# A fourth block product of an MLP layer split into seven smaller ones, on one core of a Trainium2 chip

## Chip, cores and metric

The kernel runs on one core of a Trainium2 chip. The metric is the time of one execution on the device in microseconds (us). Before the change three runs gave 829.02, 829.6 and 1758.81 us; the median is 829.6. The profile comes from a further execution of 829.24 us, with a span of 827.5 us from the first to the last instruction and a mean granted TensorE clock of 0.999.

## What is computed

An attention whose mask comes from a clustering (a query sees the keys of its own cluster), over 4 batches, 8 heads, 768 tokens and a head width of 64. Its output, 768 x 512 per batch, goes through an MLP mixer:

```python
def _moe_ref(x, w_tok1, w_tok2, w_ch1, w_ch2) -> np.ndarray:
    xt = x.transpose(0, 2, 1)
    h = np.maximum(xt @ w_tok1, 0.0) @ w_tok2      # tokens: 768 -> 256 -> 768
    u = x + h.transpose(0, 2, 1)
    h2 = np.maximum(u @ w_ch1, 0.0) @ w_ch2        # channels: 512 -> 1536 -> 512
    return (u + h2).astype(np.float32)
```

All of it is float32. The change concerns `u @ w_ch1`, the first channel product, in which 512 channels become 1536.

## The kernel before

The large products are made by Winograd's form of Strassen's scheme: both matrices are cut into 2 x 2 blocks, and seven block products stand in for eight. Sums of blocks (S1 to S4 of the left matrix, T1 to T4 of the right one) go in, and partial sums of the seven products come out. In the table, a product has the PSUM bank that it is summed up in, its two factors, and the output block that takes the bank's contents once the product is in:

```python
SEVEN = {
    "p1": ("X", "A11", "B11", "c11"),
    "p5": ("Z", "S1", "T1", "c22"),
    "c11": ("Y", "A12", "B21", "c11"),
    "u2": ("X", "S2", "T2", "c12"),
    "c12": ("Z", "S4", "B22", "c12"),
    "c22": ("X", "S3", "T3", "c22"),
    "c21": ("X", "A22", "T4", "c21"),
}
# ...
def winograd_right(b):
    yield lambda: sub(b["T1"], b["B12"], b["B11"])
    yield lambda: sub(b["T2"], b["B22"], b["T1"])
    yield lambda: sub(b["T3"], b["B22"], b["B12"])
    yield lambda: sub(b["T4"], b["B21"], b["T2"])
```

In the first channel product the left matrix is the weight, the right one is `u`, turned, so a block product is 256 channels deep and 384 tokens wide. The work is done in twelve *pairs* (four batches, three parts): a pair makes 128 rows of the upper and 128 rows of the lower half of each block (`i` is 0 or 1) by `ch1_pair`, and then the second channel product takes them in (`ch2_chunks`: 21 chunks of two matmuls of 256 columns). A whole ("big") block product of a pair is two rows x two halves of the depth, four matmuls of 384 columns. In all pairs but the first, three of the seven block products (Y = A12 B21, Z = S4 B22, X = A22 T4) are *set* products: each is cut once more, by the same table, into seven matmuls of 192 columns whose outputs are put together in SBUF.

A big product works in a bank; a chain such as Y's p1, u2, c22, c21 adds one small product after another into the same bank, and after each of them VectorE adds the bank to an output in SBUF before the next may be added to the bank.

```python
def big(psum, a, r, i, start):
    product(psum, a, r, i, start)                  # two matmuls of 384 columns
    between()                                      # hands out work that waits: sums, late chains
    if a != "A11" and beside:
        beside.pop(0)()                            # turning of the next batch's u
def set_(psum, which, name, start):                # one matmul of 192 columns
    # ...
def set_x(which, tag, name, x):
    if tag:
        chains[which] = ptile(tag, HS // 2)
    bank = chains[which]
    set_(bank, which, name, name == "p1")
    add(x, both(bank) if len(x.shape) == 3 else bank, x)
# ...
for i in range(2):
    X[i] = ptile("X", HS)
    big(X[i], "A11", "B11", i, True)
    nc.scalar.copy(out=a11[:, i], in_=X[i])
# ... (Z[0] = S1 T1, copied to p5 by ScalarE; Y's direct products c11 and c12; Y's p1)
Z[1] = ptile("Z", HS)
big(Z[1], "S1", "T1", 1, True)
nc.scalar.copy(out=p5[:, 1], in_=Z[1])
# ... (Y's u2 and p5; X[0] += S2 T2, copied to u2; Y's c22; Z's c11, c12 into Z[0])
big(X[1], "S2", "T2", 1, False)
nc.scalar.copy(out=u2[:, 1], in_=X[1])
set_x("Y", None, "c21", a11[:, 1, n0])
relu(a11)                                          # ScalarE, 768 wide
set_(Z[1][:, n0], "Z", "c21", False)
add(c12[:, 0], Z[0], u2[:, 0])
set_x("Z", "Z", "p1", c12[:, 0, n0])
add(c12[:, 1], Z[1], u2[:, 1])
big(X[0], "S3", "T3", 0, False)
add(a22[:, 0], X[0], p5[:, 0])
set_x("Z", None, "u2", c12[:, 0, n1])
set_z("Z", ptile("Y", HS // 2), c12)               # Z's p5
big(X[1], "S3", "T3", 1, False)
add(a22[:, 1], X[1], p5[:, 1])
relu(a22)
set_x("Z", None, "c22", c12[:, 1].rearrange("p (k t) -> p k t", k=2))
# ... (X's products c11, c12, c21 into X[0] and X[1], copied to a12; X's p1)
sum_1()                                            # then the second product begins;
late.extend([late_1, late_2])                      # X's u2, p5 and c22 run between its chunks
```

[...]three with the tag X, three with Z, two with Y. The kernel sets the order of the instructions on each engine itself: they stand as they are written.

Of the kernel before, what the change touches and what calls it, by code (L numbers as in the profile page):

```python
# [19 lines left out]
P = 128  # L20
# [8 lines left out]
HS = HJ * P  # L29
# [21 lines left out]
def kernel(  # L51
# [497 lines left out]

    SEVEN = {  # L550
# [16 lines left out]
    def left_weights():  # L567

        w = W["ch1"]
        half = DCH // 2  # L570
        A = pools["A"] = {
            f"A{i + 1}{j + 1}": w[:, 2 * j : 2 * j + 2, half * i : half * i + half]
            for i in range(2)
            for j in range(2)
        }
        extra = pools["wsums"].tile([P, 3, 2, half], F32, name="w1s")
        A["S1"], A["S2"], A["S4"] = (extra[:, i] for i in range(3))
        A["S3"] = A["A21"]
# [22 lines left out]
    def set_lefts():  # L601
        if "l2" not in pools:
            pools["l2"] = pools["w2sums"].tile([P, 3, 3, HS], F32, name="w1ss")
        A, l2 = pools["A"], pools["l2"]
        both = W["ch1"].rearrange("p f (i r c) -> p f i r c", i=2, r=2)[:, 2:4]
        single = A["S4"].rearrange("p f (r c) -> p f r c", r=2)
        for blocks, sums_ in (
            ([both[:, f, :, r] for r in range(2) for f in range(2)], [l2[:, 0:2, m] for m in range(3)]),
            ([single[:, f, r] for r in range(2) for f in range(2)], [l2[:, 2, m] for m in range(3)]),
        ):  # L610
            yield dict(
                zip(("A11", "A12", "A21", "A22", "S1", "S2", "S4", "S3"), blocks + sums_ + blocks[2:3])
            )
# [6 lines left out]
    def set_rights():  # L620
        uT, t4, r2 = pools["uT"], pools["R"]["T4"], pools["r2"]
        both = uT[:, :, 2:4].rearrange("p n f (k t) -> p n f k t", k=2)
        single = t4.rearrange("p f (k t) -> p f k t", k=2)
        for blocks, sums_ in (
            ([both[:, :, f, k] for f in range(2) for k in range(2)], [r2[:, 0:2, m] for m in range(3)]),
            ([single[:, f, k] for f in range(2) for k in range(2)], [r2[:, 2, m] for m in range(3)]),
        ):
            yield dict(
                zip(("B11", "B12", "B21", "B22", "T1", "T2", "T4", "T3"), blocks + sums_ + blocks[1:2])
            )  # L630

    def set_right_sums():
        pools["r2"] = pools["w2sums"].tile([P, 3, 3, HS // 2], F32, name="uTss")
        for blocks in set_rights():
            yield from winograd_right(blocks)

    def set_blocks():

        (yx, z), (yz, x) = (list(y) for y in (set_lefts(), set_rights()))
        left = {"Y": {k: a[:, 0] for k, a in yx.items()}, "X": {k: a[:, 1] for k, a in yx.items()}, "Z": z}  # L640
        right = {"Y": {k: b[:, 0] for k, b in yz.items()}, "Z": {k: b[:, 1] for k, b in yz.items()}, "X": x}
# [141 lines left out]
    def ch1_pair(part, sets, beside):  # L783
# [6 lines left out]
        p5, u2, c12 = (pools["mlp"].tile([P, 2, HS], F32, name=k) for k in ("p5", "u2", "c12"))  # L790
        A, R = pools["A"], pools["R"]
        left, right = set_blocks() if sets else (None, None)
        n0, n1 = slice(0, HS // 2), slice(HS // 2, HS)
        X, Y, Z, chains = {}, {}, {}, {}
# [15 lines left out]
        def set_(psum, which, name, start):  # L810
# [6 lines left out]
        def both(psum):  # L817
            return psum.unsqueeze(1).to_broadcast([P, 2, HS // 2])

        def relu(x):  # L820
            nc.scalar.activation(out=x, in_=x, func=ACT.Relu)  # L821


        def set_x(which, tag, name, x):
            if tag:
                chains[which] = ptile(tag, HS // 2)
            bank = chains[which]
            set_(bank, which, name, name == "p1")
            add(x, both(bank) if len(x.shape) == 3 else bank, x)

        def set_z(which, bank, x):
            set_(bank, which, "p5", True)
            add(x[:, :, n1], both(bank), x[:, :, n1])

        a11, a12, a22 = h2["A11"], h2["A12"], h2["A22"]
        for i in range(2):
            X[i] = ptile("X", HS)
            big(X[i], "A11", "B11", i, True)
            nc.scalar.copy(out=a11[:, i], in_=X[i])  # L839
        Z[0] = ptile("Z", HS)  # L840
        big(Z[0], "S1", "T1", 0, True)
        nc.scalar.copy(out=p5[:, 0], in_=Z[0])
        if sets:
            yc = ptile("X", HS)
            set_(yc[:, n0], "Y", "c11", True)
            set_(yc[:, n1], "Y", "c12", True)
            add(a11[:, 0], yc, a11[:, 0])
            set_x("Y", "Y", "p1", a11[:, 0, n0])
        Z[1] = ptile("Z", HS)
        big(Z[1], "S1", "T1", 1, True)  # L850
        nc.scalar.copy(out=p5[:, 1], in_=Z[1])
        if sets:
            set_x("Y", None, "u2", a11[:, 0, n1])
            set_z("Y", ptile("Y", HS // 2), a11)
        else:
            Y[0] = ptile("Y", HS)
            big(Y[0], "A12", "B21", 0, True)
            add(a11[:, 0], Y[0], a11[:, 0])
        big(X[0], "S2", "T2", 0, False)
        nc.scalar.copy(out=u2[:, 0], in_=X[0])  # L860
        if sets:
            set_x("Y", None, "c22", a11[:, 1, n1])
            set_(Z[0][:, n0], "Z", "c11", False)
            set_(Z[0][:, n1], "Z", "c12", False)
        else:
            Y[1] = ptile("Y", HS)
            big(Y[1], "A12", "B21", 1, True)
            add(a11[:, 1], Y[1], a11[:, 1])
        big(X[1], "S2", "T2", 1, False)
        nc.scalar.copy(out=u2[:, 1], in_=X[1])  # L870
        if sets:
            set_x("Y", None, "c21", a11[:, 1, n0])
            relu(a11)
            set_(Z[1][:, n0], "Z", "c21", False)
            add(c12[:, 0], Z[0], u2[:, 0])
            set_x("Z", "Z", "p1", c12[:, 0, n0])
            add(c12[:, 1], Z[1], u2[:, 1])
        else:
            relu(a11)
            big(Z[0], "S4", "B22", 0, False)  # L880
            add(c12[:, 0], Z[0], u2[:, 0])
        big(X[0], "S3", "T3", 0, False)
        add(a22[:, 0], X[0], p5[:, 0])
        if sets:
            set_x("Z", None, "u2", c12[:, 0, n1])
            set_z("Z", ptile("Y", HS // 2), c12)
        else:
            big(Z[1], "S4", "B22", 1, False)
            add(c12[:, 1], Z[1], u2[:, 1])
# [3 lines left out]
        if sets:  # L893
            set_x("Z", None, "c22", c12[:, 1].rearrange("p (k t) -> p k t", k=2))
            set_(X[0][:, n0], "X", "c11", False)
            set_(X[0][:, n1], "X", "c12", False)
            nc.scalar.copy(out=a12[:, 0], in_=X[0])  # L897
            set_(X[1][:, n0], "X", "c21", False)
            nc.scalar.copy(out=a12[:, 1], in_=X[1])


        def sum_3():
            nc.vector.scalar_tensor_tensor(
                out=h2["S3"], in0=c12, scalar=0.0, in1=a11, op0=ALU.max, op1=ALU.subtract
            )

        def sum_1():
            nc.vector.scalar_tensor_tensor(
                out=h2["S1"], in0=c12, scalar=0.0, in1=a22, op0=ALU.max, op1=ALU.add
            )  # L910

        def sum_4():
            sub(h2["S4"], a12, h2["S2"])

        if sets:
            set_x("X", "Y", "p1", a12[:, 0, n0])
            sum_1()

            def late_1():
                set_x("X", None, "u2", a12[:, 0, n1])  # L920
                set_z("X", ptile("Z", HS // 2), a12)
                sub(h2["S2"], h2["S1"], a11)

            def late_2():
                set_x("X", None, "c22", a12[:, 1].rearrange("p (k t) -> p k t", k=2))
                relu(a12)
                sum_3()
                sum_4()

            late.extend([late_1, late_2])  # L930
        else:
            sum_1()

            def late_(i):
                product(X[i], "A22", "T4", i, False)
                nc.scalar.activation(out=a12[:, i], in_=X[i], func=ACT.Relu)
                if i == 0:
                    sub(h2["S2"], h2["S1"], a11)
                else:
                    sum_3()  # L940
                    sum_4()

            late_(0)
            late.append(lambda: late_(1))
# [214 lines left out]
    for n, b in enumerate(batches):  # L1159
        turning = []  # L1160
        for part in range(3):
# [9 lines left out]
            if first:  # L1171
                others += list(set_right_sums()) + list(right_weights(1))
# [8 lines left out]
            if part == 2 and not last:  # L1181
                after[3] = lambda: take(turning, len(turning))
                after[15] = lambda: next(usums)
                usums = u_sums()
            ch2_chunks(b, part, last, after)
# [3 lines left out]
            if part == 2 and not last:  # L1189

                steps = list(set_right_sums())
                for m in range(2):
                    steps[m]()
                next(usums)
# [217 lines left out]
```

## Time and profile before

| what | value |
|---|---|
| time, median | 829.6 us |
| span of the profile | 827.5 us |
| TensorE busy | 818.1 us, 99% |
| VectorE busy | 605.3 us, 73% |
| ScalarE busy | 381.6 us, 46% |
| the line of the big first-channel products, L799, pX from uT | 192 records, 487 ns each |
| ReLU of the hidden blocks, L821, 768 wide | 35, 843 ns each |
| copy of a bank of 384 to SBUF, L839 | 24, 479 ns each |
| one pair with its second product, in the middle of the second batch | 35.34 us (536.86 to 572.20) |

The attention takes the first part of the span, the two channel products some 430 us at its end. In the profile, PE is TensorE, DVE VectorE, ACT ScalarE. A line number is that of the kernel before; L799 is a big product, L812 a small one, L952 the second channel product, L565 VectorE's adds, L562 its subtractions. A float32 matmul stands in the trace as two records. Matmuls are pipelined, so the length of one record is longer than the distance to the next; distances between starts tell what one costs.

### The profile page before, as it was taken

The numbers are of one execution on the slowest core, as the hardware profiler recorded it, in microseconds if no ns is written. First come the engines' busy times: TensorE is split into PE (matmuls) and PEld (weight loads), VectorE is DVE, ScalarE is ACT, GpSimd is POOL, SyncE is SP. The second block draws the span as 40 slices with busy tenths as digits, with TensorE's granted clock in tenths as the row PEclk, the third lists the DMA queues.
The fourth block names the chain that finished last, engine by engine and source line by source line (L and its number), as shares of the span: only waits on it lengthen the run. The fifth ranks groups of instructions, "written<-read, shape, count | busy, mean of one in ns | idle before, by whom it ended". The sixth has DMA issues, their size and how long they took to land.

```text
span 827.5 us, 11453 instructions
## 1 busy us (share of the span) xinstructions
PE 818.1 (99%) x4282; PEld 526.0 (64%) x4282; DVE 605.3 (73%) x1124; ACT 381.6 (46%) x562; POOL 30.6 (4%) x28
## 2 busy tenths in 40 slices
PE   8999999999999999999999999999999999999996
PEld 4444444444444444444688787878878788787875
DVE  6879898989898968859777687654677456674654
ACT  5588777787878775136202253121541214512020
POOL 1001010111101000000000000000000000000000
PEclk9999999999999999999999999999999999999999
DMA  8787676777776434143000114000130001400002
GB/s 155 141 165 145 124 141 121 160 138 154 140 155 140 84 96 121 51 156 48 0 1 1 29 34 168 1 0 15 35 105 1 1 1 30 123 1 0 1 2 80
DMA packets 184256, 63.39 MB, mean 77 GB/s; under 512 B 172800, under 2 KB 176896, under 8 KB 183936
## 3 DMA queue, kind: packets, MB, share of 16 engines
q1 hardware_dynamic: 182592, 62.18, 34.4%
q8 instruction: 35, 0.57, 0.3%
q10 hardware_dynamic: 1600, 0.39, 0.2%
q14 instruction: 29, 0.24, 0.1%
HBM read 36.21 MB, written 7.86 MB: 53 GB/s over the span
## 4 chain that ended last, share of the span: by engine, by line
PE 95%; DVE 4%; ACT 0%; issue 0%; ACTq 0%; DVEq 0%
PE sc L413 19%; PE av L455 15%; PE pX L952 14%; PE pX L799 11%; PE pZ L952 7%; PE ph L534 5%; PE pY L812 4%; PE pY L952 4%; PE pZ L799 3%; PE pZ L812 3%; PE pX L773 2%; PE pX L812 2%; PE small L491 2%; PE pZ L773 1%; PE small L304 1%; DVE hA L565 1%
## 5 line engine op out<-in xcount | busy, mean ns | idle before, releaser
L437 ACT ACTIVATE ex<-sc 128x768 f32<-128x768 f32 x192 | 151.0, 812 | 27.2 <-PE sc L413 15.5
L413 PE MATMUL sc<-qkT 64*128 64x384 f32 x768 | 155.3, 483 | 0.0
L445 DVE TENSOR_TENSOR sum<-sum,ex 128x768 f32<-128x768 f32 x128 | 127.8, 999 | 27.3 <-ACT ex L437 15.2
L455 PE MATMUL av<-ex,va 128*64 128x384 f32 x768 | 127.4, 488 | 0.0
L565 DVE TENSOR_TENSOR x<-pX,x 128x256 f32<-128x256 f32 (+1 forms) x168 | 76.2, 461 | 40.9 <-PE pX L952 40.4
L455 PEld LDWEIGHTS av<-ex,va 128*64 128x64 f32 x768 | 53.7, 137 | 71.7 <-issue 67.8
L413 PEld LDWEIGHTS sc<-qkT 64*128 64x128 f32 x768 | 67.8, 187 | 38.3 <-issue 38.0
L839 ACT COPY hA<-pX 128x384 f32<-128x384 f32 x24 | 11.5, 479 | 145.7 <-PE pX L799 145.7
L565 DVE TENSOR_TENSOR hA<-pY,hA 128x192 f32<-128x192 f32 (+1 forms) x90 | 36.8, 409 | 49.9 <-PE pY L812 36.0
L821 ACT ACTIVATE hA<-hA 128x768 f32<-128x768 f32 x35 | 29.5, 843 | 87.1 <-DVE hA L565 87.1
L799 PE MATMUL pX<-uT,wc 128*128 128x384 f32 x192 | 67.9, 487 | 0.0
L413 PE MATMUL sc<-ohT 64*128 64x384 bf16 x384 | 62.4, 323 | 0.0
L799 PEld LDWEIGHTS pX<-uT,wc 128*128 128x128 f32 x192 | 35.7, 190 | 17.5 <-issue 0.6
L462 ACT COPY avrows<-av 128x768 uint16<-128x768 uint16 x32 | 25.6, 799 | 44.1 <-PE av L455 44.1
L565 DVE TENSOR_TENSOR x<-pZ,x 128x256 f32<-128x256 f32 (+1 forms) x84 | 36.6, 459 | 11.9 <-PE pZ L952 11.8
L534 PE MATMUL ph<-x,wt 128*128 128x512 f32 x96 | 41.6, 593 | 0.0
L413 PEld LDWEIGHTS <-ohT 64*128 64x128 bf16 x384 | 18.7, 94 | 33.9 <-issue 9.6
L952 PE MATMUL pX<-wc,hA 128*128 128x256 f32 x144 | 36.9, 380 | 0.4 <-ACT hA L897 0.4
L708 ACT COPY uT<-ucols 128x768 uint16<-128x768 uint16 x32 | 33.3, 1052 | 4.5 <-DMA ucols<-urows 4.5
L952 PE MATMUL pY<-wc,hA 128*128 128x256 f32 x144 | 35.1, 379 | 0.0
L952 PE MATMUL pZ<-wc,hS 128*128 128x256 f32 x144 | 35.0, 379 | 0.0
L799 PE MATMUL pX<-uTs,w1s 128*128 128x384 f32 x96 | 34.9, 486 | 0.0
(178 smaller groups left out, 1266.7 us busy)
## 6 DMA issues: line engine op xcount, KB each, us to landing
raw<-in_moe_w_ch_dram SPq DMA_DIRECT2D x24, 512.0 KB, 4.4
va<-in_v_dram SPq DMA_DIRECT2D x16, 384.0 KB, 3.6
out_dram<-x SPq DMA_DIRECT2D x24, 256.0 KB, 2.5
qk<-in_k_dram SPq DMA_DIRECT2D x60, 96.0 KB, 3.8
qk<-in_q_dram SPq DMA_DIRECT2D x60, 96.0 KB, 3.5
raw<-in_moe_w_tok_dram SPq DMA_DIRECT2D x3, 512.0 KB, 4.3
raw<-in_moe_w_tok_dram SPq DMA_DIRECT2D x4, 384.0 KB, 3.9
spill<-x SPq DMA_DIRECT2D x1, 1536.0 KB, 5.1
```

Of the source, the lines that this page charges most:

```text
L413: nc.tensor.matmul(sc[:, h, 0:HS], lhsT=src[rows, 1, j], rhs=src[rows, 0, HJ * qh : HJ * qh + HJ], start=start, stop=not start,)
L437: nc.scalar.activation(out=ex, in_=sc[:, :, 0:HS], func=ACT.Exp, scale=SM_SCALE)
L445: nc.vector.tensor_tensor(out=acc, in0=acc if j > 1 else st["ex", qh, 0], in1=st["ex", qh, j], op=ALU.add)
L455: nc.tensor.matmul(av[h * D : (h + 1) * D], lhsT=st["va"][:, h, j], rhs=ex[:, h], start=(j == 0), stop=(j == NJ - 1),)
L462: nc.scalar.copy(out=st["rows"][:, qh], in_=av.bitcast(U16).rearrange("p (t w) -> p w t", w=2))
L534: nc.tensor.matmul(pf, lhsT=W["tok1"][:, j, t * P : (t + 1) * P], rhs=xs[b][:, j], start=(j == 0), stop=(j == NJ - 1),)
L565: nc.vector.tensor_tensor(out=dst, in0=a, in1=b, op=ALU.add)
L708: nc.scalar.copy(out=out, in_=pools.pop(("ucols", i)).rearrange("p w j t -> p w (j t)"))
L799: nc.tensor.matmul(psum, lhsT=A[a][:, k, c], rhs=R[r][:, k], start=start and k == 0, stop=k == 1, skip_group_check=not start,)
L812: nc.tensor.matmul(psum, lhsT=left[which][a][:, part * P : part * P + P], rhs=right[which][r], start=start, stop=True, skip_group_check=no ...
L821: nc.scalar.activation(out=x, in_=x, func=ACT.Relu)
L952: nc.tensor.matmul(psum, lhsT=h2[a][:, k, i * P : (i + 1) * P], rhs=Bw[w][:, part + 3 * k], start=start and k == 0, stop=k == 1, skip_grou ...
```

## The change

S1 T1 was a big product: two rows, two halves of the depth, four matmuls of 384 columns, collected in a bank Z[i] that went on to take Z's direct products. It becomes a fourth set product, called P: seven matmuls of 192 columns, put together in SBUF in `p5`. The aim is the same as with the other three: one eighth less of matmul columns for that block product. P needs the sums of its own blocks (of S1 on the left, of T1 on the right), so the tiles of the small sums grow from three to four sets. Since Z and P can't use S1 T1's bank any more, the output c12 starts from X (after S2 T2) plus `p5`, added by VectorE, where ScalarE copied X to `u2` before; and the order of the pair's products is new, so that the steps of two chains (Y and P, then Z) alternate with big products.

The core of the diff (the restructuring that moves the pair without sets into its own function, and the parts that are kept under new names, are left out):

```diff
     def set_lefts():
-            pools["l2"] = pools["w2sums"].tile([P, 3, 3, HS], F32, name="w1ss")
+            pools["l2"] = pools["w2sums"].tile([P, 4, 3, HS], F32, name="w1ss")
 ...
+        pz = pools["w1s"][:, 0:3:2].rearrange("p i f (r c) -> p f i r c", r=2)
+        for n, both in enumerate((yx, pz)):
 ...
     def set_rights():
 ...
+        x, p = (R[name].rearrange("p f (k t) -> p f k t", k=2) for name in ("T4", "T1"))
         for blocks, sums_ in (
 ...
+            ([p[:, f, k] for f in range(2) for k in range(2)], [r2[:, 3, m] for m in range(3)]),
 ...
     def ch1_pair(part, sets, beside):
-        p5, u2, c12 = (pools["mlp"].tile([P, 2, HS], F32, name=k) for k in ("p5", "u2", "c12"))
+        p5, c12 = (pools["mlp"].tile([P, 2, HS], F32, name=k) for k in ("p5", "c12"))
 ...
+    def ch1_sets(part, product, big, relu, a11, a12, a22, p5, c12, sum_1, sum_2, sums_34):
 ...
+        X = [ptile("X", HS), None]
+        big(X[0], "A11", "B11", 0, True)
+        nc.scalar.copy(out=a11[:, 0], in_=X[0])
+        ybe = ptile("Y", HS)
+        direct(ybe, "Y")
+        add(a11[:, 0], ybe, a11[:, 0])
+        X[1] = ptile("X", HS)
+        big(X[1], "A11", "B11", 1, True)
+        nc.scalar.copy(out=a11[:, 1], in_=X[1])
+        pbe = ptile("Z", HS)
+        direct(pbe, "P")
+        nc.scalar.copy(out=p5[:, 0], in_=pbe)
+        yq, pq = ptile("Y", HS), ptile("Z", HS)
+        chain(yq, "Y", "p1", a11[:, 0, n0])
+        chain(pq, "P", "p1", p5[:, 0, n0])
         big(X[0], "S2", "T2", 0, False)
+        chain(yq, "Y", "u2", a11[:, 0, n1])
+        yz, pz = ptile("X", HS), ptile("Z", HS)
+        column(yz, "Y", a11)
+        chain(pq, "P", "u2", p5[:, 0, n1])
+        small(pz[:, n0], "P", "p5")
+        nc.scalar.copy(out=p5[:, 1, n1], in_=pz[:, n0])
+        add(p5[:, 0, n1], pz[:, n0], p5[:, 0, n1])
+        add(c12[:, 0], X[0], p5[:, 0])
         big(X[1], "S2", "T2", 1, False)
-        nc.scalar.copy(out=u2[:, 1], in_=X[1])
+        chain(yq, "Y", "c22", a11[:, 1, n1])
+        chain(pq, "P", "c22", p5[:, 1, n1])
+        direct(ybe, "Z")
+        chain(yq, "Y", "c21", a11[:, 1, n0])
+        relu(a11)
+        small(pq[:, n0], "P", "c21", False)
+        nc.scalar.copy(out=p5[:, 1, n0], in_=pq[:, n0])
+        add(c12[:, 0], ybe, c12[:, 0])
+        add(c12[:, 1], X[1], p5[:, 1])
+        chain(yz, "Z", "p1", c12[:, 0, n0])
         big(X[0], "S3", "T3", 0, False)
         add(a22[:, 0], X[0], p5[:, 0])
+        chain(yz, "Z", "u2", c12[:, 0, n1])
+        column(pbe, "Z", c12)
         big(X[1], "S3", "T3", 1, False)
         add(a22[:, 1], X[1], p5[:, 1])
         relu(a22)
+        chain(yz, "Z", "c22", c12[:, 1, n1])
+        direct(X[0], "X", False)
+        nc.scalar.copy(out=a12[:, 0], in_=X[0])
+        chain(yz, "Z", "c21", c12[:, 1, n0])
+        small(X[1][:, n0], "X", "c21", False)
+        nc.scalar.copy(out=a12[:, 1], in_=X[1])
+        chain(yq, "X", "p1", a12[:, 0, n0])
+        sum_1()
 ...
             if part == 2 and not last:
                 after[3] = lambda: take(turning, len(turning))
-                after[15] = lambda: next(usums)
+                after[15] = first_sums                     # T1, and the list of the small sums
+                after[17] = lambda: (steps[2][0](), steps[2][1]())   # P's first two right sums
 ...
-                others += [lambda m=m: (steps[m](), steps[m + 1]()) for m in (2, 4, 6)]
+                others.append(lambda: [step() for step in (yz[2], p[2], yz[3], p[3])])
+                others += [lambda: None, lambda: [step() for step in x]]
```

`chain` is one small matmul into the chain's bank and VectorE's add of that bank to an output, `direct` two small matmuls (c11 and c12) into the two halves of a bank, `column` the small p5 and its add to two outputs. `others` is the list from which `between` takes one entry after each big product.

More of the change, by code (lines that the diff above doesn't have):

```diff
@@ L575, in left_weights @@
         }
-        extra = pools["wsums"].tile([P, 3, 2, half], F32, name="w1s")
+        extra = pools["w1s"] = pools["wsums"].tile([P, 3, 2, half], F32, name="w1s")
         A["S1"], A["S2"], A["S4"] = (extra[:, i] for i in range(3))
@@ L602, in set_lefts @@
         if "l2" not in pools:
-            pools["l2"] = pools["w2sums"].tile([P, 3, 3, HS], F32, name="w1ss")
[L604 to L610, printed above, removed]
+            pools["l2"] = pools["w2sums"].tile([P, 4, 3, HS], F32, name="w1ss")
+        l2 = pools["l2"]
+        yx = W["ch1"].rearrange("p f (i r c) -> p f i r c", i=2, r=2)[:, 2:4]
+        pz = pools["w1s"][:, 0:3:2].rearrange("p i f (r c) -> p f i r c", r=2)
+        for n, both in enumerate((yx, pz)):
+            blocks = [both[:, f, :, r] for r in range(2) for f in range(2)]
+            sums_ = [l2[:, 2 * n : 2 * n + 2, m] for m in range(3)]
             yield dict(
@@ L620, in set_rights @@
     def set_rights():
-        uT, t4, r2 = pools["uT"], pools["R"]["T4"], pools["r2"]
-        both = uT[:, :, 2:4].rearrange("p n f (k t) -> p n f k t", k=2)
-        single = t4.rearrange("p f (k t) -> p f k t", k=2)
+        uT, R, r2 = pools["uT"], pools["R"], pools["r2"]
+        yz = uT[:, :, 2:4].rearrange("p n f (k t) -> p n f k t", k=2)
+        x, p = (R[name].rearrange("p f (k t) -> p f k t", k=2) for name in ("T4", "T1"))
         for blocks, sums_ in (
-            ([both[:, :, f, k] for f in range(2) for k in range(2)], [r2[:, 0:2, m] for m in range(3)]),
-            ([single[:, f, k] for f in range(2) for k in range(2)], [r2[:, 2, m] for m in range(3)]),
+            ([yz[:, :, f, k] for f in range(2) for k in range(2)], [r2[:, 0:2, m] for m in range(3)]),
+            ([x[:, f, k] for f in range(2) for k in range(2)], [r2[:, 2, m] for m in range(3)]),
+            ([p[:, f, k] for f in range(2) for k in range(2)], [r2[:, 3, m] for m in range(3)]),
         ):
@@ L632, in set_right_sums @@
     def set_right_sums():
-        pools["r2"] = pools["w2sums"].tile([P, 3, 3, HS // 2], F32, name="uTss")
-        for blocks in set_rights():
-            yield from winograd_right(blocks)
+        pools["r2"] = pools["w2sums"].tile([P, 4, 3, HS // 2], F32, name="uTss")
+        return [list(winograd_right(blocks)) for blocks in set_rights()]
     def set_blocks():
-        (yx, z), (yz, x) = (list(y) for y in (set_lefts(), set_rights()))
-        left = {"Y": {k: a[:, 0] for k, a in yx.items()}, "X": {k: a[:, 1] for k, a in yx.items()}, "Z": z}
-        right = {"Y": {k: b[:, 0] for k, b in yz.items()}, "Z": {k: b[:, 1] for k, b in yz.items()}, "X": x}
+        (yx, pz), (yz, x, p) = (list(y) for y in (set_lefts(), set_rights()))
+        left = {name: {k: a[:, i] for k, a in two.items()} for two, i, name in
+                ((yx, 0, "Y"), (yx, 1, "X"), (pz, 0, "P"), (pz, 1, "Z"))}
+        right = {"Y": {k: b[:, 0] for k, b in yz.items()}, "Z": {k: b[:, 1] for k, b in yz.items()},
+                 "X": x, "P": p}
         return left, right
@@ L789, in ch1_pair @@
         }
-        p5, u2, c12 = (pools["mlp"].tile([P, 2, HS], F32, name=k) for k in ("p5", "u2", "c12"))
+        p5, c12 = (pools["mlp"].tile([P, 2, HS], F32, name=k) for k in ("p5", "c12"))
         A, R = pools["A"], pools["R"]
-        left, right = set_blocks() if sets else (None, None)
-        n0, n1 = slice(0, HS // 2), slice(HS // 2, HS)
-        X, Y, Z, chains = {}, {}, {}, {}
+        a11, a12, a22 = h2["A11"], h2["A12"], h2["A22"]
         def product(psum, a, r, i, start):
@@ L808, in big, with relu, sum_1, sum_2 @@
                 beside.pop(0)()
-        def set_(psum, which, name, start):
+        def relu(x):
+            nc.scalar.activation(out=x, in_=x, func=ACT.Relu)
+        def sum_1():
+            nc.vector.scalar_tensor_tensor(
+                out=h2["S1"], in0=c12, scalar=0.0, in1=a22, op0=ALU.max, op1=ALU.add
+            )
+        def sum_2():
+            sub(h2["S2"], h2["S1"], a11)
+        def sums_34():
+            nc.vector.scalar_tensor_tensor(
+                out=h2["S3"], in0=c12, scalar=0.0, in1=a11, op0=ALU.max, op1=ALU.subtract
+            )
+            sub(h2["S4"], a12, h2["S2"])
+        (ch1_sets if sets else ch1_plain)(
+            part, product, big, relu, a11, a12, a22, p5, c12, sum_1, sum_2, sums_34
+        )
+    def ch1_plain(part, product, big, relu, a11, a12, a22, p5, c12, sum_1, sum_2, sums_34):
+        X, Z = {}, {}
+        for i in range(2):
+            X[i] = ptile("X", HS)
+            big(X[i], "A11", "B11", i, True)
+            nc.scalar.copy(out=a11[:, i], in_=X[i])
+        for i in range(2):
+            Z[i] = ptile("Z", HS)
+            big(Z[i], "S1", "T1", i, True)
+            nc.scalar.copy(out=p5[:, i], in_=Z[i])
+        for i in range(2):
+            Y = ptile("Y", HS)
+            big(Y, "A12", "B21", i, True)
+            add(a11[:, i], Y, a11[:, i])
+            big(X[i], "S2", "T2", i, False)
+            nc.scalar.copy(out=c12[:, i], in_=X[i])
+        relu(a11)
+        for i in range(2):
+            big(Z[i], "S4", "B22", i, False)
+            add(c12[:, i], Z[i], c12[:, i])
+            big(X[i], "S3", "T3", i, False)
+            add(a22[:, i], X[i], p5[:, i])
+        relu(a22)
+        sum_1()
+        def late_(i):
+            product(X[i], "A22", "T4", i, False)
+            nc.scalar.activation(out=a12[:, i], in_=X[i], func=ACT.Relu)
+            (sums_34 if i else sum_2)()
+        late_(0)
+        late.append(lambda: late_(1))
+    def ch1_sets(part, product, big, relu, a11, a12, a22, p5, c12, sum_1, sum_2, sums_34):
+        left, right = set_blocks()
+        n0, n1 = slice(0, HS // 2), slice(HS // 2, HS)
+        def small(psum, which, name, start=True):
             _, a, r, _ = SEVEN[name]
@@ L815, in set_ @@
             )
[L817 to L858, printed above, removed]
-        big(X[0], "S2", "T2", 0, False)
[L860 to L868, printed above, removed]
@@ L869, in ch1_pair, with direct @@
-        big(X[1], "S2", "T2", 1, False)
-        nc.scalar.copy(out=u2[:, 1], in_=X[1])
[L871 to L881, printed above, removed]
+        def direct(bank, which, start=True):
+            small(bank[:, n0], which, "c11", start)
+            small(bank[:, n1], which, "c12", start)
@@ new lines, in chain, with column @@
+        def chain(q, which, name, x):
+            small(q[:, n0], which, name, name == "p1")
+            src = q[:, n0]
+            if len(x.shape) == 3:
+                src = src.unsqueeze(1).to_broadcast([P, 2, HS // 2])
+            add(x, src, x)
+        def column(z, which, x):
+            small(z[:, n0], which, "p5")
+            add(x[:, :, n1], z[:, n0].unsqueeze(1).to_broadcast([P, 2, HS // 2]), x[:, :, n1])
+        X = [ptile("X", HS), None]
+        big(X[0], "A11", "B11", 0, True)
@@ L882, in ch1_pair @@
+        direct(ybe, "Z")
+        chain(yq, "Y", "c21", a11[:, 1, n0])
+        relu(a11)
+        small(pq[:, n0], "P", "c21", False)
[3 more added lines that the diff above has]
+        chain(yz, "Z", "p1", c12[:, 0, n0])
         big(X[0], "S3", "T3", 0, False)
         add(a22[:, 0], X[0], p5[:, 0])
[L884 to L889, printed above, removed]
+        chain(yz, "Z", "u2", c12[:, 0, n1])
@@ L892, in ch1_pair, with late_1, late_2 @@
         relu(a22)
[L893 to L944, printed above, removed]
+        chain(yz, "Z", "c22", c12[:, 1, n1])
[5 more added lines that the diff above has]
+        chain(yq, "X", "p1", a12[:, 0, n0])
+        sum_1()
+        def late_1():
+            chain(yq, "X", "u2", a12[:, 0, n1])
+            column(pz, "X", a12)
+            sum_2()
+        def late_2():
+            chain(yq, "X", "c22", a12[:, 1].rearrange("p (k t) -> p k t", k=2))
+            relu(a12)
+            sums_34()
+        late.extend([late_1, late_2])
     def ch2_chunks(b, part, last, after=()):
@@ L1171 @@
             if first:
-                others += list(set_right_sums()) + list(right_weights(1))
+                others += sum(set_right_sums(), []) + list(right_weights(1))
             if n == 0 and part == 1:
@@ L1182, with first_sums @@
                 after[3] = lambda: take(turning, len(turning))
-                after[15] = lambda: next(usums)
                 usums = u_sums()
+                steps = []
+                def first_sums():
+                    next(usums)
+                    steps.extend(set_right_sums())
+                after[15] = first_sums
+                after[17] = lambda: (steps[2][0](), steps[2][1]())
             ch2_chunks(b, part, last, after)
@@ L1189 @@
             if part == 2 and not last:
-                steps = list(set_right_sums())
-                for m in range(2):
-                    steps[m]()
+                yz, x, p = steps
+                yz[0]()
+                yz[1]()
                 next(usums)
                 others += [lambda: next(usums)] * 2
-                others += [lambda m=m: (steps[m](), steps[m + 1]()) for m in (2, 4, 6)]
+                others.append(lambda: [step() for step in (yz[2], p[2], yz[3], p[3])])
+                others += [lambda: None, lambda: [step() for step in x]]
                 if n == 0:
```

## The prediction

> **What bounds the kernel now.** I read the page's busy shares and its chain first:
>
> ```profile
> PE 818.1 (99%) x4282; PEld 526.0 (64%) x4282; DVE 605.3 (73%) x1124; ACT 381.6 (46%) x562; POOL 30.6 (4%) x28
> ...
> PE 95%; DVE 4%; ACT 0%; issue 0%; ACTq 0%; DVEq 0%
> ```
>
> TensorE is busy for 99% of the span and is 95% of the chain. So a matmul removed is worth its spacing, and a wait of TensorE costs its full length. Next, the order of time in a typical pair (third part of the second batch; columns: start us, length us, engine, line, operation, count; one float32 matmul is two records):
>
> ```profile
> 536.86 2.74 PE L799 MATMUL pX<-uT,wc 128*128 128x384 f32 x8
> 539.44 1.45 PE L799 MATMUL pZ<-uTs,w1s 128*128 128x384 f32 x4
> 540.73 0.49 PE L812 MATMUL pX<-uT,wc 128*128 128x192 f32 x2
> 541.06 0.49 PE L812 MATMUL pX<-uT,w1ss 128*128 128x192 f32 x2
> ...
> 547.20 0.49 PE L812 MATMUL pY<-uTss,wc 128*128 128x192 f32 x2
> 547.53 0.49 PE L812 MATMUL pZ<-uTss,w1s 128*128 128x192 f32 x2
> 547.73 0.36 DVE L565 TENSOR_TENSOR hA<-pY,hA 128x192 f32<-128x192 f32 x1 [1.91 <-PE pY L812]
> 547.85 0.49 PE L812 MATMUL pZ<-uT,w1s 128*128 128x192 f32 x2
> 548.00 0.55 DVE L565 TENSOR_TENSOR c<-pZ,u 128x384 f32<-128x384 f32 x1
> 548.18 1.45 PE L799 MATMUL pX<-uT,wc 128*128 128x384 f32 x4
> 548.18 0.84 ACT L821 ACTIVATE hA<-hA 128x768 f32<-128x768 f32 x1 [0.30 <-DVE hA L565]
> 548.65 0.36 DVE L565 TENSOR_TENSOR c<-pZ,c 128x192 f32<-128x192 f32 x1
> ...
> 549.47 0.49 PE L812 MATMUL pZ<-uTss,w1ss 128*128 128x192 f32 x2
> ...
> 552.20 0.84 ACT L821 ACTIVATE hA<-hA 128x768 f32<-128x768 f32 x1 [3.18 <-DVE hA L565]
> 552.95 0.46 ACT L897 COPY hA<-pX 128x384 f32<-128x384 f32 x1
> 553.03 1.03 PE L952 MATMUL pX<-wc,hA 128*128 128x256 f32 x4
> ```
>
> Starts, not lengths, give the cost: two 384-wide matmuls (x4) take 540.73-539.44 = 1.29, so 0.645 each; a 192-wide one 541.06-540.73 = 0.325. The next pair starts at 572.20, so the period is 35.34. It holds 16 x 0.645 + 21 x 0.325 + 42 x 0.4325 (256-wide) = 35.31: **there is no wait to speak of**. Any wait that the new order brings is new time.
>
> Waits do exist at the start of a new batch, where VectorE makes the sums of the new right sides:
>
> ```profile
> 505.99 1.45 PE L799 MATMUL pZ<-uTs,w1s 128*128 128x384 f32 x4
> 507.14 0.36 DVE L565 TENSOR_TENSOR hA<-pY,hA 128x192 f32<-128x192 f32 x1
> 507.55 0.92 PE L812 MATMUL pY<-uTss,w1ss 128*128 128x192 f32 x4
> 508.31 1.45 PE L799 MATMUL pX<-uTs,w1s 128*128 128x384 f32 x4
> ```
>
> The u2 of Y was due at 505.99+1.29 = 507.28 and ran at 507.55, 0.05 after the VectorE add (507.14+0.36) that it waits for. The two matmuls then took 0.76 instead of 0.65. So a wait costs its length plus about 0.1 for restarting.
>
> **What the Trainium skill says.** "FP8 and Floating Point Precision", TensorE Precision Notes: true float32 takes four passes. An estimate from it, 4 x 384 / 2.4 GHz = 0.640, agrees with 0.645. "TensorE: Matmul & The Clock Gate", the table under its title: VectorE and ScalarE queues are strict FIFO, TensorE only pulls weight loads ahead. The trace agrees: no instruction of either engine overtakes. "ScalarE: Activation LUTs", What ACT_TABLE_LOAD costs: back-to-back ACTIVATEs overlap by about 93 ns. Here the copy at 552.95 starts 0.75 after an 0.84 ReLU, so 0.09. "Perfetto Trace Analysis", Identifying the Most-Contended Engine: matmul busy share doesn't show the distance from the limit. Agrees: the 0.27 wait above lies beside PE records that leave no gap.
>
> **The change part by part**, for the 11 pairs that use set products (the first pair stays plain).
>
> *Removed and added on TensorE.* S1T1 was 2 rows x 2 = 4 matmuls of 384: 4 x 0.645 = 2.58. It becomes 7 of 192: 2.275. Gain 0.305 a pair, 3.4 in all, which would give 826.2.
>
> *VectorE.* P adds p1, u2, p5, c22 (4 x 0.36), X0+p5 becomes an add of 0.55 instead of a ScalarE copy, and Z's c22 is split from one 0.55 into 2 x 0.36: about 2.2 a pair, on an engine busy 19.7 of 35.3 (busy time in the stretch 536.86 to 572.20). In sum that fits. P's right sums add 4 x 0.35 per batch; the left sums of P widen 12 instructions from 0.29 (128) to 0.42 (256), 1.6 once (durations from the groups by shape). These are mostly beside the long second product.
>
> *The order.* I laid the new order on TensorE's clock with t = 0 at the pair's start, using the latencies above: a 192 matmul can be read 0.53 after its start (547.20 to 547.73), VectorE to ScalarE 0.09 (548.09 to 548.18), to TensorE 0.05, ScalarE to VectorE 0.03. A 192 copy on ScalarE is an estimate of 0.30, extrapolated from 0.479 (384) and 0.843 (768). Without waits TensorE runs X0 0, Y's c11 and c12 1.29, X1 1.94, P's two 3.23, Y p1 3.88, P p1 4.20, S2T2 4.53, Y u2 5.82, Y p5, P u2, P p5 to 7.12, S2T2 to 8.41, Y c22, P c22, Z's c11 and c12 to 9.71, Y c21 9.71, P c21 10.035, Z p1 10.36, S3T3 10.685, Z u2 11.975. Up to there every chained matmul has slack (the tightest are the c21's, 0.36).
>
> Z u2 adds into the bank that VectorE reads for Z p1, so it needs that add to be done. The way to it, from Y c21: 9.71 + 0.53 = 10.24 VectorE add to 10.60; relu(a11) on ScalarE from 10.69. The copy of P c21 stands behind this ReLU in ScalarE's queue although its data is there at 10.57: it starts 0.75 later, 11.44, and ends 11.74. VectorE's next but one, X1 + p5[1], needs it: 11.77 to 12.32. Z's p1 add stands behind that: 12.24 to 12.60. So Z u2 runs at 12.65, not 11.975: **a wait of 0.68**, plus 0.1 for restarting. In the kernel before there was no ScalarE step in this chain (548.00 and 548.65 follow each other on VectorE while the ReLU runs beside them).
>
> After that everything shifts: S3T3 of the second row 13.41, Z c22 14.70 (readable 15.23). Its add waits behind a22's (14.90 to 15.46) and ends 15.74; Z c21 stands at 15.675 and needs 15.79: 0.12 plus some 0.05 for restarting. X c21 16.19, X p1 16.51, first matmul of the second product 16.84. Before it was 553.03-536.86 = 16.17. Sum for a pair: -0.305 + 0.78 + 0.17 = +0.65, or 16.84-16.17 = +0.67.
>
> *New batches* (3 of the 11). The wait of 0.27+0.1 disappears: Y p1's add, behind the sums, ends at 5.12, and Y u2 is due only at 5.82. But X's four right sums (4 x 0.35) are put between Z's p1 add and a22's: Z u2's add comes at 14.27, Z c22's at 15.69 to 16.05, so Z c21 waits 0.43 and not 0.12. First matmul of the second product 17.15, before 517.69-501.14 = 16.55: +0.60. Two more adds (0.35 each) at the end of the batch's last chunks fit into VectorE's gaps of 0.44 per chunk.
>
> Sum: 8 x 0.67 + 3 x 0.60 = 7.2. 829.6 + 7.2 = **836.8**.
>
> **Rivals.**
> *A, no wait takes hold: 826.2 (-0.4%).* That needs the add of Z p1 0.7 earlier. For it speaks that I have a 192 copy only as an estimate. Against: even a copy of no length at all would leave 0.38 of the wait, because of the ReLU's 0.75.
> *B, VectorE becomes the bound: 840 or more.* For it: 2.2 more per pair, and it is in nearly every chain; a delay at one add moves all that follow. Against: 22 of 36 busy, and in the second product it sits idle 0.44 before each add.
> *C, only the big wait comes: 829.6 + 11 x (0.78 - 0.305) = 834.8.* The second wait hangs on 0.12, less than I can vouch for in my sum of latencies.
> *D, the eight PSUM banks* are all held between S2T2's start and the pair's end (3 X, 3 Z, 2 Y). A late release could block the first chunks of the second product. Against: its first bank is that of Z's chain, free at about 16.73, just before 16.84. It would add up to 0.1 a pair: 838.
>
> **Range and chances.** B, C and D lie between 834 and 840; A is unlikely. I take 836.5, range 832.5 to 840. 2% is 16.6 us, five times the gain on TensorE and more than double my loss; so faster 0.005, within 0.98, slower 0.015.
>
> **What would show it.** Right: in the order of time of a middle pair, Z u2 starts 1.8 to 2.2 after S3T3 and not 1.29; just before, ScalarE's 192 copy starts straight after relu(a11) and VectorE waits for it before X1 + p5[1]; the pair's start to the second product's first matmul is 16.7 to 16.9 instead of 16.17. The 192 matmuls still come at 0.325. Wrong: Z u2 follows S3T3 at 1.29 (then A), or waits sit at Y's or P's chain (then my order of VectorE's work is off), or the second product itself grows beyond 42 x 0.4325.

## Result and the profile after

The changed kernel takes 836.43 us (836.21 to 836.69, 6 runs), the kernel before 829.53; the ratio is 1.0086 with a 95% interval of 1.0072 to 1.0100. So it is slower by 0.9%, though TensorE has fewer matmul columns to stream. One execution of the kernel before took 1758.81 us; it is left out of the ratio, and 829.53 is the median with it.

From the page of the changed kernel, busy shares and the chain that ended last (the work followed back from the last instruction, at each step to what released it):

```profile
PE 820.4 (98%) x4348; PEld 534.5 (64%) x4348; DVE 631.0 (76%) x1206; ACT 372.2 (45%) x551; POOL 30.7 (4%) x28
...
PE 95%; DVE 2%; ACT 1%; issue 1%; ACTq 0%; DVEq 0%
```

TensorE's busy share has gone from 99% to 98%, and ScalarE and "issue" (time in which an engine waits for nothing that the profile shows) have entered the chain with 1% each, where they had 0%; VectorE's share of it went from 4% to 2%. The records fit the edit: 66 more on TensorE (11 pairs x 3 more matmuls x 2 records), 82 more on VectorE (11 x 6 + 4 batches x 4), 11 fewer on ScalarE. TensorE's waits from 400 us on were a list of two single entries before; now there is one that comes in each pair (columns: engine, tile and line, for whom it waited; us in total, times, longest):

```profile
PE pX L873 <- DVE c L566: 5.6, 11, 0.5
```

Eleven times, once in each pair with set products. The profile counts 0.5 each time, from the modelled end of the matmul before; the distances between starts give 0.67. The order of time in the pair that answers to the one shown before (third part of the second batch; it starts at 539.05):

```profile
549.08 0.49 PE L873 MATMUL pZ<-uTss,w1s 128*128 128x192 f32 x2
549.28 0.36 DVE L566 TENSOR_TENSOR hA<-pY,hA 128x192 f32<-128x192 f32 x1 [0.62 <-PE pY L873]
...
549.73 1.45 PE L800 MATMUL pX<-uT,wc 128*128 128x384 f32 x4
549.74 0.84 ACT L812 ACTIVATE hA<-hA 128x768 f32<-128x768 f32 x1 [3.05 <-DVE hA L566]
550.49 0.30 ACT L925 COPY p<-pZ 128x192 f32<-128x192 f32 x1
550.82 0.56 DVE L566 TENSOR_TENSOR c<-pX,p 128x384 f32<-128x384 f32 x1 [0.71 <-ACT p L925]
551.29 0.35 DVE L566 TENSOR_TENSOR c<-pX,c 128x192 f32<-128x192 f32 x1
551.70 0.59 PE L873 MATMUL pX<-uTss,w1ss 128*128 128x192 f32 x2 [0.51 <-DVE c L566]
552.12 0.49 PE L873 MATMUL pZ<-uTss,w1ss 128*128 128x192 f32 x2
...
553.94 0.56 DVE L566 TENSOR_TENSOR hA<-pX,p 128x384 f32<-128x384 f32 x1 [0.60 <-PE pX L800]
...
554.39 0.49 PE L873 MATMUL pX<-uTs,w1ss 128*128 128x192 f32 x2
554.42 0.35 DVE L566 TENSOR_TENSOR c<-pX,c 128x192 f32<-128x192 f32 x1
554.53 0.84 ACT L812 ACTIVATE hA<-hA 128x768 f32<-128x768 f32 x1 [3.75 <-DVE hA L566]
...
554.82 0.59 PE L873 MATMUL pX<-uTss,w1s 128*128 128x192 f32 x2
...
555.28 0.46 ACT L938 COPY hA<-pX 128x384 f32<-128x384 f32 x1
...
555.57 0.49 PE L873 MATMUL pY<-uTs,wc 128*128 128x192 f32 x2
...
555.92 0.73 PEld L963 LDWEIGHTS pX<-wc,hA 128*128 128x128 f32 x4 [0.16 <-ACT hA L938]
555.95 1.10 PE L963 MATMUL pX<-wc,hA 128*128 128x256 f32 x4
```

To be read from top to bottom: P's c21 starts at 549.08 and can be read by 549.61 (0.53 later, as in the prediction). ScalarE is idle then, but relu(a11), which stands ahead of the 192-wide copy in its queue, has to wait for VectorE's add to a11 (549.28) and starts at 549.74; the copy follows it at 550.49. VectorE stands idle for 0.71 until the copy is there for its add of X1 and p5[1] (550.82), then adds Z's p1 (551.29), and only then may Z's u2 start: 551.70, where 549.73 + 1.29 = 551.02 was due (0.67 late before rounding). The matmul after it comes 0.42 later and not 0.325, so 0.10 more goes to restarting.

The lines from 553.94 on show two smaller losses at the pair's end. VectorE takes a22's add (553.94) before Z's c22 add (554.42), so Z's c21 is due at 554.39 + 0.325 = 554.71 and starts at 554.82; restarting costs 0.10 again. And on ScalarE the copy of a12's first row (555.28) stands behind relu(a22) (554.53). The weight load of the second product's first matmul waits for that copy, by the profile's account. This matmul doesn't read a12, so what it waits for must be the PSUM bank that the copy empties. It is due at 555.57 + 0.325 = 555.90 and starts at 555.95, and what follows its two matmuls of 256 columns comes a further 0.08 late (at 556.89, after 0.94 and not 0.865).

The starts of the pairs in the order of time show where the 6.9 us lie:

| distance from a pair's start to the next | before | after |
|---|---|---|
| middle pairs (5 of them) | 35.34 | 36.08 |
| first pair of a batch (3rd and 4th batch; the 2nd is 35.72 and 36.28) | 35.71 | 36.28 |
| the two with sets in the first batch | 36.04, 35.44 | 36.57, 36.19 |
| the last pair, up to the last VectorE add | 36.11 | 36.71 |

From the first pair with sets to the last VectorE add it is 821.10 - 429.66 = 391.44 before and 828.72 - 430.01 = 398.71 after: 7.27 more. The first of these pairs starts 0.35 later, no more than this start differs among the traces of the runs below (429.09 to 430.15), and the write-out behind the last add is 0.5 shorter in this profile, which brings the spans to 7.1 apart.

### The profile page after: what moved, and what is told of

Read it like the earlier page. It is cut to its first block, busy times and chain, and to the rows that moved or that the text cites. A ratio compares the mean times of both kernels' runs of the same rounds, so it can differ in the third digit from the quotient of the medians.

```text
span 834.6 us, 11693 instructions
## 1 busy us (share of the span) xinstructions
PE 820.4 (98%) x4348; PEld 534.5 (64%) x4348; DVE 631.0 (76%) x1206; ACT 372.2 (45%) x551; POOL 30.7 (4%) x28
## 4 chain that ended last, share of the span: by engine, by line
PE 95%; DVE 2%; ACT 1%; issue 1%; ACTq 0%; DVEq 0%
PE sc L413 19%; PE av L455 15%; PE pX L963 15%; PE pX L800 9%; PE pZ L963 7%; PE ph L534 5%; PE pY L873 5%; PE pY L963 4%; PE pZ L873 3%; PE pX L873 3%; PE pX L776 2%; PE small L491 2%; PE pZ L776 1%; PE small L304 1%; DVE c L566 1%
## 5 line engine op out<-in xcount | busy, mean ns | idle before, releaser
L800 PE MATMUL pX<-uT,wc 128*128 128x384 f32 x192 | 69.7, 487 | 0.0
L896 ACT COPY hA<-pX 128x384 f32<-128x384 f32 x11 | 5.3, 479 | 132.5 <-PE pX L800 132.5
```

Source lines behind the costliest of these rows:

```text
L800: nc.tensor.matmul(psum, lhsT=A[a][:, k, c], rhs=R[r][:, k], start=start and k == 0, stop=k == 1, skip_group_check=not start,)
```

## Experiments

My theory was: the saved matmul columns are there, but a chain of queue orders (relu(a11), then P's copy behind it on ScalarE, then VectorE's adds) makes TensorE wait once in each pair, and a smaller order of adds makes it wait again at the pair's end. The rivals: VectorE simply has too much to do in the pair; or the added copy costs it wherever it stands.

### The copy ahead of the ReLU

```diff
-        relu(a11)
         small(pq[:, n0], "P", "c21", False)
         nc.scalar.copy(out=p5[:, 1, n0], in_=pq[:, n0])
+        relu(a11)
```

> The changed kernel with one thing moved: ScalarE's copy of P's c21 stands before relu(a11), not after it. Theory (the copy behind the ReLU in ScalarE's queue holds VectorE, and so Z's u2): Z's p1 add ends at about 11.82 after the pair's start and Z's u2 is due at 11.975, so the wait of 0.66 and its restart of 0.11 go, less some 0.05 of a late weight load: 0.72 x 11 = 7.9, about 828.5. Rival 1 (VectorE has too many adds in the pair, the ReLU only stands beside it): nothing changes, 836. Rival 2 (the added copy itself costs it, wherever it stands): about 0.3 of the 0.77 stays, 832.

Measured: 827.82 us against 829.04 of the kernel before on the same chip, ratio 0.9984 (0.9977 to 0.9991). That is 8.6 less than the changed kernel (8.1 when each is held against the kernel before in its own set of runs: 6.9 above it and 1.2 below); 7.9 was expected. From the start of the first pair with sets to the last VectorE add, the traces differ by 398.71 - 390.05 = 8.66. In the order of time of the same pair:

```profile
546.38 0.49 PE L873 MATMUL pZ<-uTss,w1s 128*128 128x192 f32 x2
...
546.90 0.32 ACT L924 COPY p<-pZ 128x192 f32<-128x192 f32 x1 [2.92 <-PE pZ L873]
547.03 1.45 PE L800 MATMUL pX<-uT,wc 128*128 128x384 f32 x4
547.12 0.85 ACT L812 ACTIVATE hA<-hA 128x768 f32<-128x768 f32 x1
547.32 0.55 DVE L566 TENSOR_TENSOR c<-pX,p 128x384 f32<-128x384 f32 x1
547.78 0.35 DVE L566 TENSOR_TENSOR c<-pX,c 128x192 f32<-128x192 f32 x1
548.32 0.49 PE L873 MATMUL pX<-uTss,w1ss 128*128 128x192 f32 x2
```

The copy now comes 0.52 after its matmul's start, VectorE doesn't wait for it, and Z's u2 follows S3T3 at 548.32 - 547.03 = 1.29, its bare spacing. The work of all three engines is the same as in the changed kernel; so neither the amount of VectorE's work nor the copy itself was the cause. Most of the 0.7 over expectation fits the 0.05 a pair that I had set aside for a late weight load, which didn't come (11 x 0.05 = 0.55).

### VectorE's order instead of ScalarE's

```diff
-        add(c12[:, 1], X[1], p5[:, 1])
         chain(yz, "Z", "p1", c12[:, 0, n0])
+        add(c12[:, 1], X[1], p5[:, 1])
```

> The changed kernel with one thing moved on VectorE and none on ScalarE: Z's p1 add stands before the add of X1 and p5[1], which waits for the copy. Theory (a chain by queue order): the wait and its restart go although the copy comes as late as before; 0.77 x 11 = 8.5, about 828.0, and VectorE still sits idle some 0.6 before the add of X1 and p5[1]. Rival 1 (VectorE's amount of work): 836, the amount is the same. Rival 2 (the copy costs it by itself): 836, or 832 at best.

Measured: 829.39 us, ratio to before 1.0006 (0.9997 to 1.0014). The copy still stands behind the ReLU:

```profile
547.46 0.36 DVE L566 TENSOR_TENSOR c<-pX,c 128x192 f32<-128x192 f32 x1
547.74 0.30 ACT L925 COPY p<-pZ 128x192 f32<-128x192 f32 x1
548.07 0.56 DVE L566 TENSOR_TENSOR c<-pX,p 128x384 f32<-128x384 f32 x1 [0.25 <-ACT p L925]
548.27 0.49 PE L873 MATMUL pX<-uTss,w1ss 128*128 128x192 f32 x2
```

Z's p1 add (547.46) has gone ahead, and Z's u2 starts without a wait, so this second place where the chain can be cut works as well. VectorE waits 0.25 for the copy and not the 0.6 that I wrote, since the add that went ahead fills part of it. The time is 1.4 worse than expected. The trace shows where: in the new batches VectorE, having waited for the copy, has X's right sums and a22's add still before it, and there Z's c22 waits 0.39 and takes 0.10 to restart (in the second batch it is due at 512.92 + 1.29 = 514.21 and starts at 514.60), which the kernel with the copy ahead doesn't have. Three times 0.49 are 1.5, and 829.39 - 827.82 = 1.57.

### The ReLU twice, after and before

```diff
         relu(a11)
+        relu(a11)
```

> The changed kernel with relu(a11) done twice in each pair with sets (the second does nothing to the values). Theory: the ReLU's length is in the chain, so the wait at Z's u2 grows by the 0.75 by which two ReLUs follow each other: 0.75 x 11 = 8.3, about 844.7. Rival 1 (VectorE's amount of work): unchanged at 836.4. Rival 2 (the copy's own length): unchanged at 836.4.

> The kernel before with relu(a11) done twice in each pair with sets. Theory: there the ReLU is in no chain of TensorE's, ScalarE is idle for 3 us after it, so nothing changes: 829.5, ratio 1.000 within 0.001. If a longer ReLU costs time by itself (by the SBUF it reads, or through the second product's start), 830 or more.

Measured: after the change 845.84 us, 9.4 above the changed kernel; in the kernel before 829.15, ratio 1.0001 (0.9992 to 1.0010). In the changed kernel's variant:

```profile
552.03 1.72 ACT L812 ACTIVATE hA<-hA 128x768 f32<-128x768 f32 x2 [3.05 <-DVE hA L566]
553.66 0.30 ACT L926 COPY p<-pZ 128x192 f32<-128x192 f32 x1
553.99 0.56 DVE L566 TENSOR_TENSOR c<-pX,p 128x384 f32<-128x384 f32 x1 [1.59 <-ACT p L926]
```

The same instruction is free in one kernel and costs its full length in the other. The wait at Z's u2 is 1.55 there and 0.67 in the changed kernel: 0.88 more in each of 11 pairs, 9.7 in all. My 0.75 was too small: the two ReLUs take 1.72, so the second starts 0.88 after the first, while 0.75 assumed that they overlap. Why they don't is not shown. The second reads what the first wrote; but the exponentials of the attention, each on a tile of its own, hardly overlap either (starts 0.81 apart at a length of 0.81).

### The end of the pair

```diff
-        add(a22[:, 1], X[1], p5[:, 1])
-        relu(a22)
         chain(yz, "Z", "c22", c12[:, 1, n1])
+        add(a22[:, 1], X[1], p5[:, 1])
         direct(X[0], "X", False)
         nc.scalar.copy(out=a12[:, 0], in_=X[0])
+        relu(a22)
         chain(yz, "Z", "c21", c12[:, 1, n0])
+        chain(yq, "X", "p1", a12[:, 0, n0])
         small(X[1][:, n0], "X", "c21", False)
         nc.scalar.copy(out=a12[:, 1], in_=X[1])
-        chain(yq, "X", "p1", a12[:, 0, n0])
         sum_1()
```

> The changed kernel with the end of the pair in another order: on VectorE Z's c22 add stands before a22's second row; on TensorE X's p1 comes before X's c21; on ScalarE the copy of a12's first row comes before relu(a22). Theory (Z's c21 waits 0.11, in new batches 0.30, plus 0.11 for restarting, because Z's c22 add stands behind a22's): this wait goes but for a late weight load of about 0.05, while the wait of 0.66 at Z's u2 stays: 8 x 0.17 + 3 x 0.35 = 2.4, about 834.0. Rival (the two waits are one: the second is only the wake of the first): 836.4.

Measured: 833.91 us, ratio 1.0052 (1.0038 to 1.0065), 2.5 less than the changed kernel (2.0 when each is held against its own kernel before; in the traces the stretch of the pairs is 398.71 - 395.78 = 2.93 shorter). The wait of 0.67 at Z's u2 is still there in each pair, so the second wait was not its wake.

The run moves three things at once, though, and its trace shows two effects where I expected one. At Z's c21 a middle pair lost 0.20, and 0.07 is left, at the matmul after it. The second product's first matmul, which lost 0.13, now follows without a delay (554.96 - 554.64 = 0.32): the copy of a12's first row runs ahead of relu(a22), at 554.12. (Z's c21 add, which ends next to that copy in the changed kernel, is not what held it: here the weight load starts at 554.80, before this add ends at 554.88.) So a middle pair is 0.27 shorter (35.81), about half of it by each. In the last pair, on the other hand, TensorE waits 0.75 for the second product to begin, where it was 0.49. It is partly luck that the sum came so near to the expected 2.4. Both edits together:

> The changed kernel with both: the copy of P's c21 ahead of relu(a11), and the new end of the pair. Theory (the two waits are separate and are all that keeps the saved matmul columns from showing): 827.8 less 8 x 0.17 + 3 x 0.33 = 2.4, about 825.4, so 0.4% under the kernel before. Rival (TensorE has some further cost of 192-wide matmuls that the spacing of 0.325 doesn't show): it stays at 827 or more.

Measured: 825.06 us, ratio 0.9946 (0.9933 to 0.9960).

```profile
550.13 0.49 PE L873 MATMUL pX<-uTs,wc 128*128 128x192 f32 x2
550.33 0.36 DVE L566 TENSOR_TENSOR c<-pX,c 128x192 f32<-128x192 f32 x1 [0.78 <-PE pX L873]
550.45 0.49 PE L873 MATMUL pX<-uTs,w1ss 128*128 128x192 f32 x2
550.60 0.55 DVE L566 TENSOR_TENSOR hA<-pX,p 128x384 f32<-128x384 f32 x1
550.78 0.56 PE L873 MATMUL pX<-uTss,w1s 128*128 128x192 f32 x2
```

Z's c22 add (550.33) now goes ahead of a22's (550.60), and Z's c21 starts at 550.78, 0.33 after the matmul before it. What is left is 0.07 at the next one. The time is below the 827 of the rival, so the 192-wide matmuls have no further cost of that size.

### X's right sums in two halves

```diff
-                others += [lambda: None, lambda: [step() for step in x]]
+                others += [lambda: None, lambda: (x[0](), x[1]()), lambda: (x[3](), x[2]())]
```

> As the one with both, and in a new batch X's four right sums are given out in two halves, two after S3T3's first row and two after its second, where all four came after the first. Theory: the four sums hold up Z's u2 and c22 adds in the three new batches by some 0.6, of which 0.1 to 0.3 reaches TensorE: 0.2 to 0.6 us less than with both, about 825.0. Otherwise equal.

Measured with all three edits: 824.59 us, ratio to before 0.9941 (0.9928 to 0.9955). Against the version without it that is 0.5 less, but the two intervals overlap, and in the trace only the 0.10 that is lost at one matmul of each new batch has become 0.07, 0.1 us in all. So the third edit is worth no more than that, as far as these runs show; I had given it 0.2 to 0.6. Two starts of pairs in its order of time:

```profile
535.60 1.45 PE L800 MATMUL pX<-uT,wc 128*128 128x384 f32 x4
...
570.63 1.45 PE L800 MATMUL pX<-uT,wc 128*128 128x384 f32 x4
```

The period is 35.03, and 12 x 0.645 + 28 x 0.325 + 42 x 0.4325 = 35.005 is what the matmuls need. This version beats both kernels. It is 829.05 - 824.59 = 4.5 under the kernel before, and the saved columns account for 11 x 0.305 = 3.4 of that. Most of the rest comes from the new order: the kernel before lost 0.27 + 0.10 at Y's u2 in the first pair of three batches (35.71 there), which this one doesn't (35.04).

## Why the prediction was right, step by step

The time was 836.43 for a predicted 836.5, and 11 pairs cost 7.27 for a predicted 7.2.

- *Gain on TensorE, 0.305 a pair.* Right, and shown by the last version: 35.34 - 35.03 = 0.31. "No wait to speak of" was nearly right: the kernel before lost 0.06 in each pair, at X's u2 between the chunks of the second product (554.28 - 553.89 = 0.39 for 0.325), and the last version loses 0.07 elsewhere.
- *The wait of 0.68 at Z's u2.* Measured 0.67 and 0.10 for restarting, as worked out. All stations up to there came within 0.05 of the plan: the ReLU at 549.74 - 539.05 = 10.69 (planned 10.69), the copy at 11.44 (11.44), X1 + p5[1] at 11.77 (11.77), Z's p1 add at 12.24 (12.24), Z's u2 at 12.65 (12.65). The estimate of 0.30 for a 192 copy was 0.30. That the cause is the order of the queues, and not the amount of work, is shown by moving one line in either of two queues, and by the doubled ReLU.
- *The second wait, 0.12 at Z's c21.* Measured 0.11, and gone, with the loss named next, in the run with the other end of the pair. Its restart was 0.10, not 0.05.
- *A third loss, left out of the plan.* The first matmul of the second product was 0.05 late and took 0.08 to restart, because a copy stood behind a ReLU once more. With the longer restart above, this makes the start of the second product 555.95 - 539.05 = 16.90 where 16.84 was planned, and the middle pair's cost 0.74 where it was 0.67 (the 0.06 that the kernel before lost is gone in exchange).
- *New batches, +0.60.* Measured 0.55 to the start of the second product (519.87 - 502.77 = 17.10, before 16.55). The wait at Z's c21 was 0.30 there, not 0.43: X's sums and the adds behind them went by a little faster on VectorE than I had laid out (Z's u2 add started 14.17 after the pair's start where I had 14.27, Z's c22 add 15.56 where I had 15.69). This miss and the two above are of opposite sign, so it is luck that the sum came out better than its terms.
- *Rivals.* A (no wait, 826.2) was nearly what the version with both edits reached, but not what stood in the program. B (VectorE as the bound) fell with the moved copy; VectorE was busy for 21.72 of the pair's 36.08. C, without the second wait, would be 834.8; the run without it gave 833.91, but the third loss was gone there too. D (banks) did come, in small: it is the third loss, 0.13 a pair where up to 0.1 was allowed, and the bank is, by the profile's account, the one that the copy of a12's first row empties, not that of Z's chain.
- *A reading that was off.* The prediction says that the PE records leave no gap at the wait of 0.27. They leave 507.55 - (505.99 + 1.45) = 0.11, less than half of the wait.

What stays open is the size of the restart: after a wait the next start comes 0.08 to 0.10 late, and 0.06 to 0.07 where the release falls just ahead of its slot. I read it as a weight load that isn't made in advance. The trace fits: at Z's u2 the weight load starts 0.01 before its matmul (551.69), at the next big product 0.16 before (552.29 for 552.45). No run tests it.

## What to carry to other kernels

Where TensorE's spacing leaves no gap, count the waits that a new order brings as carefully as the matmuls that it saves: here 0.31 saved a pair stood against 0.82 of waits in three places and 0.28 of restarts, less the 0.06 that the old order lost. Such a wait can be found on paper from the distances in the old trace, by following each engine's queue in program order and asking for each short operation which long one stands ahead of it. It has to be asked for each of them: the copy behind the second ReLU of the pair was missed here. The cure costs one line: put the short copy that others wait for ahead of the long ReLU whose result is needed only later, and let an add whose data is there go before one that must still wait.

## What I had not expected of the hardware

Two ReLUs on the same tile follow each other after 0.88 us, while a copy of another tile follows a ReLU after 0.75; whether it is the repetition in place that loses the overlap was not tested. And the plan on paper held to within a few hundredths over twelve microseconds, so latencies between engines are steady enough here (0.53 from a 192-wide matmul's start to its reader, 0.03 to 0.10 from VectorE or ScalarE to another engine) to be added up.
